# Sliding-window attention into a gated FFT convolution: the inverse transform's complex residues folded about the middle of a block

## The chip, the core and the metric

One core of a Trainium2 chip runs the whole program. The metric is the device time of one execution in microseconds (us), less being better. A core has TensorE (PE in the profile, with its weight loads as PEld), VectorE (DVE), ScalarE (ACT), GpSimd (POOL) and SyncE (SP); each takes its own instructions in order, and they wait for one another by semaphores. In this kernel POOL mostly issues the DMAs that load, and SP those that store or transpose.

## What is computed

Four batches of 768 positions, 8 heads of 64 channels. Each head attends to the last 96 positions and to the first 8, with a bias that falls linearly with distance; its output, as 768 x 512, goes through a projection to three parts x1, x2, x3; x2 is convolved circularly over the 768 positions with a filter, by a Fourier transform; the result is gated by x1 and x3 and projected again.

```python
scores = scale * np.matmul(q, k.transpose(0, 1, 3, 2))
...
a = np.exp(scores)
a = a / (np.sum(a, axis=-1, keepdims=True) + 1e-09)
return np.matmul(a, v).astype(np.float32)
...
proj = x @ w_proj
x1, x2, x3 = (proj[..., :D], proj[..., D:2 * D], proj[..., 2 * D:])
X2 = np.fft.rfft(x2, n=S, axis=1)
H = np.fft.rfft(filter_fft, n=S, axis=0)[None, :, :]
x2_conv = np.fft.irfft(X2 * H, n=S, axis=1)
y = x1 * x2_conv * x3
return (y @ w_out).astype(np.float32)
```

## The kernel before

**Order.** Every piece of work is an operation of a plan (`Plan.op`), and the text `ORDER` writes out the order of all of them by hand: `382P3` is operation 382 on PE into PSUM bank 3, `383A` operation 383 on ACT, V is DVE, G is POOL, S is SP. Many operations may stand on either ACT or DVE (copies out of PSUM, scalings), and the text says which. Words such as `i1b4` are idle products: one 128x512 product (`busy`, L313) whose result nobody reads, put in bank 4. There are 12 of them among the first 66 words and 6 at the very end. The engines follow this order blindly; what is late delays all that stands behind it on its engine.

**Attention, batch b** (`attention`). For batch 0, heads come in pairs: q and k of a pair are loaded, turned on PE (`turned_pair`, L742) and copied to QT and KT. `scores` puts the products of q and k (L809) in two banks; ACT takes their exponential (L821). In batch 0 the bias is added by PE itself (`biased`, L592 to L599, with tables `near` and `edge` that POOL and DVE make from the distances `dg`); in batches 1 to 3 DVE multiplies by a mask (L838). `values` multiplies with v (L857, L862), DVE takes reciprocals (L886) and scales (L881; on ACT L885, in 8 pieces), and x is transposed (PE, L909; batch 3: by DMA, L896). `gate` multiplies with the weights of x1 and x3 (L962, L964), copies x1 out (L321 or L323) and forms g = x1 x3: either ACT copies x3 out first (L976) and DVE multiplies in SBUF, or DVE multiplies straight from PSUM (L978, two forms).

**Convolution, batch b** (`conv`). The transform of 768 positions is split by hand: DVE sums and differences (`butterfly`, L927 to L946) make a real residue and complex residues, `proj` (L1038) multiplies them with the weights of x2, `forward` (L714) with tables `fwd` of sines and cosines, and `spectra` multiplies with the filter's spectrum (L1217 to L1234). The inverse goes, for each of 4 blocks of 128 channels (jp, jj) and for even and odd frequencies (par), through one bank: two products of 256 columns with the tables `inv` (the complex residue, L1066), added up in PSUM, and two of 128 columns with `inr` (the real residue z, L1066 and L1069). The 384 columns are copied to the tile `eo` (ACT L317, mostly). Then `mixed` (DVE, five operations L1168 to L1172, one of which, L1169, may stand on ACT) turns z, u, w into three thirds of a half block, `gated` joins even and odd ones (L1186, L1187) and multiplies by g (L1197), and `out` (L1100) projects; the result is copied (L321 or L323) and stored (L1107). For batches 0 to 2 `mixed` works on all 4 blocks at once (1024 elements per partition), for the last batch on two (512).

**Tables.** `tables` makes the sines: PE forms angles (L503 to L510), ACT and DVE reduce them (L438 to L444), ACT takes the sine (L447). `inverse_tables` transposes six tables on PE (L519, L522) and copies them, scaled, to `inv` and `inr` (six operations on ACT or DVE).

Of the kernel before, what the change touches and what calls it, by code (L numbers as in the profile page):

```python
# [41 lines left out]
0V 3G 14S i1b0 11V 26G i1b1 5V 10V 31G 215P0 7V 1V i1b2 29G 8V 15A i1b3 216A 28G 16V 210P1 217V 13V 6G 218V i1b4 25G  # L42
4V 2A 53V 20V 211A 70P0 27G 9A 212V 100P2 24G 213V 219A i1b5 30G 71V 101A 86P1 44G 84P3 220V 214A i1b6 221V i1b7 85A
87V 18G 58P2 i1b4 i1b0 72P3 12V 21G i1b5 19V 17S i1b1 49V 56P1 255G 50V 202A 54V 52V 73A 51V 92P45 88V 47V 102V 89P67
22G 57A 32G 74V 45V 90P 48V 93P 59V 91A 98P3 33G 75P01 94A 23V 46V 78P67 99V 35G 76P 60A 79P 77A 55V 64P45 36G 61P23
230V 80A 65P 34G 62P 106P01 66A 231V 95P67 38G 63A 96P 107P 232V 103P45 37G 108A 67P23 233V 68P 40G 97A 104P 234V
109P01 222V 39G 105A 235V 112P67 110P 257G 69A 81P45 113V 114V 82P 111A 42G 117P23 236V 127P67 118V 200A 265G 119V
201A 237P0 83A 244P1 128V 264G 129V 122P23 245A 157P45 238A 123V 41G 124V 115P1 130P0 158V 256G 116A 152P67 159V 198A
203A 239P1 254G 131A 153V 125P4 154V 199A 160P5 120P0 253G 223P2 161V 121A 126V 155P3 271G 224V 250P67 156A 143P0 225V
262G 252A 189V 382P3 197A 183V 196A 133P7 263G 251A 209V 190V 142P4 383A 269G 182V 138P6 206V 144A 208V 270G 353P3  # L50
135A 355P4 184V 140A 145V 226V 137P5 43G 356V 227A 354A 351P6 192V 268G 178P4 246A 146V 240A 228V 172P3 487G 139V 241A
247P01 352V 486G 147P5 248A 229V 249V 380P6 174A 258G 149A 148P7 381V 384A 357A 180A 132P5 267G 185V 150A 141V 429P4
186V 134A 273G 191V 367P67 364P01 430V 394P23 368A 167P5 493G 187V 193V 395A 431P4 188V 293P6 194V 500G 204V 169A 195V
365A 177P7 432V 499G 151V 294A 391P45 207V 388P01 385P23 369V 392A 261G 289P6 433V 179V 386A 259S 427P4 266G 290V
278P5 389A 260S 428V 494G 205V 358P67 361P23 396V 437P01 359A 492G 276P4 279V 438A 393V 291P6 274G 277V 362A 173P7
501G 366V 292A 387V 443P23 175A 440P45 272G 434P01 363V 444A 280P6 360V 485G 441A 390V 584P7 370P23 176V 435A 483G
439V 302P4 168P5 303A 495G 402P01 585A 170V 136V 371V 372V 658P4 403V 436V 484G 397P23 281A 404V 609P7 659A 491G 163P6
398V 171V 375P01 445V 498G 165A 162P5 399V 610A 660P4 497G 442V 304P6 446P23 164A 376V 586A 377V 305A 488G 400P5 284P7
447V 401V 378P6 719G 448V 285A 451P01 661A 611P7 181V 727G 379A 452V 449P4 453V 612A 580P5 724G 582P6 450V 373P2 581A
454P3 374V 502G 405P7 662V 242P4 455V 613A 406A 656P2 583V 734G 295P5 166V 657A 297P7 476V 296A 716G 623P23 489S  # L60
593P01 243A 477V 282P6 594A 730G 417P4 490S 298V 624A 407P5 720S 715G 419V 413P7 283A 300V 496G 409A 478V 620P23
663P01 415A 617P45 621A 479V 729G 422P6 306V 412P7 664A 503G 595V 467P2 618A 480V 713G 418P3 424A 414V 469A 714G
596P45 287V 614P67 666P01 597A 665V 522P2 504G 420V 286V 615A 423P4 421V 732G 523A 717S 518P5 299V 667A 718S 275G 598V
590P23 425A 587P67 307V 669P01 731G 519A 509P4 622V 588A 733G 301V 461P5 510A 426V 288V 591A 725G 672P67 408P4 668V
673A 723G 505P2 416V 481V 670A 589V 728G 316P3 320P6 482V 506A 322P7 726G 671V 321A 604P01 308P2 463A 605V 318P6 410V
323A 606V 712G 457P5 317A 592V 309A 314P7 319A 674V 310P3 459A 312P2 619V 315A 533P6 599P01 625V 534A 722G 507P5 600V
311A 411V 601A 313V 735G 680P67 616V 472P4 840S 681V 682V 631P23 474A 626P01 508A 812S 632V 324V 607P6 633A 471P7 325V
456P5 627V 839S 326V 466P4 608V 628A 327V 511P6 838S 513P2 328V 520P3 329V 458A 841S 514A 675P01 521A 330V 683P5 512A
815S 526P3 468A 676V 462P2 677V 527A 531P4 813S 464A 634P6 331V 629P3 684A 602P0 339P2 630A 532V 887S 473A 678P1 332V
524P3 333P7 814S 525A 635V 603V 679A 336P6 516V 340A 811S 705V 334A 845P01 842P23 848P45 846A 460V 342P7 884S 529V  # L70
849A 470V 646P0 465V 843A 847V 885S 636P1 343V 337A 819P23 816P45 535V 648A 886S 641P7 820A 528V 647P0 817A 721S 701P6
649V 475V 530V 638A 650V 345P2 703A 844V 643A 536V 825P01 346A 851P67 888P45 515V 826A 695P3 517V 652P2 889A 706V
686P0 852A 545P1 827V 688A 891P45 708V 822P67 697A 651P0 546A 821V 823A 541P3 707V 696P1 892A 653V 547P6 824V 637P7
548A 709V 698A 549P4 639A 539P5 818V 833P01 542A 710V 537P7 540A 834V 543P3 711V 550A 642P6 544A 538A 828P45 644V 835V
645V 836S 348P3 829V 640V 830A 853V 753P6 344S 654V 893V 551P7 850V 751P0 754A 655V 832S 552A 859P45 349A 553V 854P67
752A 831S 691P3 860V 554V 861A 555V 700P2 350S 855V 685P0 556V 347S 690P1 856V 702A 687A 699V 897P45 862S 557V 894P67
757P0 895A 689V 749P2 558V 837S 898A 755P6 560V 750A 736P7 857S 890V 764P2 737A 740P4 899V 756A 863S 561V 738P5 741A
559V 758A 900P67 341S 693A 858S 896V 765A 577P0 759V 739A 905P23 338S 901V 578A 902V 335S 692A 762P5 742P4 763A 704V
865P1 903S 906V 760V 574P5 867A 907V 904S 744P1 575A 761V 571P0 743A 766V 909S 745A 568P5 572A 746V 565P4 908S 694V
767V 562P0 747V 770P1 748V 563A 774P2 778P3 569A 864P0 930V 566A 570S 772P5 779A 579S 869P4 931V 573S 773A 567S 874P3  # L80
871A 564S 866A 768P5 933V 576S 776P4 780P0 932V 777A 782P6 775A 868V 926P7 934V 783A 781A 941P2 935V 771A 936V 769A
954P6 942A 784V 950P5 955A 785V 786V 952P2 951A 787V 937P6 953V 939P5 788V 938A 876A 789V 965P4 940A 958P6 963P3 959A
791V 956P2 915P5 957A 964A 916P6 961V 966A 943P3 960V 875P2 967V 945P4 962V 920P1 946A 968V 944A 870P0 928A 984P4 947V
877A 880P3 985A 948V 988P2 872A 879P4 949V 989A 975P0 878V 881A 873V 986P2 790V 982P7 917A 971P4 918A 910P5 882V 987A
883V 983A 969P6 972A 973P3 990V 911P7 919V 974A 991V 976A 921P4 913V 992V 970A 792V 922A 925P0 912A 977V 802P1 923A
993V 978A 914V 805P4 927A 994V 979V 929V 808P0 980V 806A 924V 803A 981V 807S 799P7 1010V 809A 1008V 796P6 810S 800A
804S 1009V 793P0 1011V 797A 798S 1015P1 794A 997V 801S 995V 795S 1018P6 1016A 1021P7 996V 1017S 1012P1 998V 1022A
1019V 1005P0 1020S 1013V 1023S 999P6 1014S 1006V 1002P7 1007S 1000V i1b2 1001S 1003A i1b5 i1b3 i1b4 1004S i1b1 i1b0
# [112 lines left out]
class Fused:  # L201
# [12 lines left out]
    DF = ()  # L214
    DI = ()
# [26 lines left out]
    def buffers(self):  # L242
# [23 lines left out]
        self.inv = t("inv", [P, 4, 2, P])  # L266
# [11 lines left out]
        self.eo = t("eo", [P, 4, 2, S // 2])  # L278
# [6 lines left out]
        self.mix = t("mix", [P, 4, 2, P])  # L285
# [3 lines left out]
        self.fwt = t("fwt", [P, 9, P]) if self.DF else None  # L289
        self.fws = t("fws", [P, 10, P]) if self.DF else None  # L290
        self.ivt = t("ivt", [P, 4, 3, P]) if self.DI else None
        self.irt = t("irt", [P, 2, 3, P]) if self.DI else None
        spare = self.eo.rearrange("p a b c -> p (a b c)")
        flat = self.mix.rearrange("p a b c -> p (a b c)")
        self.idle, self.far = flat[:, 0:512], flat[:, 512:728]
        self.edge = flat.bitcast(BF16)[:, 728:896]
# [5 lines left out]
        self.row = spare[0:1, 1984:2624].rearrange("p (a b) -> p a b", a=5)  # L302
# [5 lines left out]
        self.th = [th[:, 0:512], th[:, 512:768]]  # L308
# [78 lines left out]
    def setup(self):  # L387
# [21 lines left out]

        def ident(_):  # L410
            make_identity(nc, self.ident)
# [17 lines left out]
    def tables(self):  # L429

        nc, g, S = self.nc, self.g, self.S
        nf = 2.0 * math.pi / S * (1.0 - 4.0e-7)
        for a, n in enumerate((512, 256)):
            b = g.bank()
            g.op("P", 0.5 if a == 0 else 0.3, lambda _, a=a, b=b: self.angles(a, b.f32()),
                 r=["rows", "irow"], acq=[b], name="angles")
# [479 lines left out]
    def butterfly(self, js):  # L916
# [20 lines left out]
        if self.b in self.DF:  # L937
            return
# [446 lines left out]
```

## Time and profile before

| | us |
|---|---|
| time, median of 3 runs (lowest to highest) | 171.12 (170.71 to 171.39) |
| the profiled execution | 168.81 |
| its span, first to last instruction | 167.1 |
| ACT: exponentials L821, 48 of 920 ns | 40.1 |
| PE: gate products L962, 192 of 326 ns | 36.0 |
| DVE: masks L838, 36 of 597 ns | 20.7 |
| PE: complex residues of the inverse L1066, 64 of 272 ns | 11.4 |
| DMA while POOL loads, 40 to 60 us | 156 to 157 GB/s |

A line such as `L1066 PE MATMUL bank<-inv,X 128*128 128x256 f16 x64 | 11.4, 272` gives the line, the engine, what is written and read, the shape, how many there were, the time that they were busy in all, and the mean ns of one. Products overlap: the time from one start to the next is less than the ns of one. The chain of waits lists what the end waited for, in order of time (start, length, what), and there a group of products has the time from its first start to the next one's.

### The profile page before, as it was taken

To read this page: it belongs to the slowest core of one execution; us is meant where nothing else is said; L and a number is where in the kernel's file an instruction comes from. 1 tells how busy PE (TensorE), PEld (TensorE's weight loads), DVE (VectorE), ACT (ScalarE), POOL (GpSimd) and SP (SyncE) were. 2 spreads that over 40 slices of the span, in tenths; PEclk is the share of its full clock that TensorE was granted. 3 is DMA by queue.
4 is the path that set the end of the run, shared out by engine and by line. 5 is a ranking of instruction groups with operands and counts; after the bars stand their busy time and mean duration, and the time that the engine had idled before them with its cause. 6 is when DMAs were issued, how large, how long until landed. Compare 5 with 4: busy or idle time off the path is not lost.

```text
span 167.1 us, 4421 instructions
## 1 busy us (share of the span) xinstructions
PE 161.8 (97%) x1710; PEld 101.0 (60%) x1710; DVE 151.7 (91%) x345; ACT 141.7 (85%) x290; POOL 74.5 (45%) x96
## 2 busy tenths in 40 slices
PE   6899999999999999999999999999999999999993
PEld 1355588766557785557767556756454754685451
DVE  6965989899999999999999999999997999889980
ACT  7757999899999899999999899988886786698821
POOL 8989598897899999997400000000000000000000
PEclk9999999999999999999999999999999999999999
DMA  2999999999999999999996551024245460000595
GB/s 25 165 194 205 152 177 172 167 154 189 149 155 160 153 150 158 148 160 167 151 152 111 71 108 30 4 78 156 52 144 147 158 246 2 0 4 2 200 346 209
DMA packets 90365, 22.44 MB, mean 134 GB/s; under 512 B 81504, under 2 KB 87400, under 8 KB 90344
## 3 DMA queue, kind: packets, MB, share of 16 engines
q0 software_dynamic: 75296, 12.85, 98.0%
q1 hardware_dynamic: 15048, 9.31, 20.7%
q8 instruction: 13, 0.21, 0.5%
q14 instruction: 8, 0.07, 0.1%
HBM read 25.69 MB, written 6.29 MB: 191 GB/s over the span
## 4 chain that ended last, share of the span: by engine, by line
PE 90%; DMA 5%; POOL 2%; ACT 1%; SPq 0%; issue 0%; POOLq 0%
PE bank L962 19%; PE bank L1100 12%; PE bank L1038 12%; PE bank L809 7%; PE bank L964 6%; PE bank L714 6%; PE bank L1066 5%; PE bank L857 4%; DMA qn<-in_q_dram 3%; PE bank L783 3%; PE bank L862 3%; PE bank L909 3%; PE bank L313 2%; PE bank L592 2%; PE bank L742 2%; DMA xT<-xn 1%
## 5 line engine op out<-in xcount | busy, mean ns | idle before, releaser
L821 ACT ACTIVATE E<-bank 128x864 f16<-128x864 f32 x48 | 40.1, 920 | 1.6 <-PE bank L809 1.5
L962 PE MATMUL bank<-xT,w 128*128 128x384 f16 x192 | 36.0, 326 | 0.0
L333 POOL DMA_DIRECT2D vn<-in_v_dram x28 | 26.4, 957 | 2.4 <-DMA g<-in_moe_filter_fft_dram 1.4
L962 PEld LDWEIGHTS <-w 128*128 128x128 f16 x192 | 17.7, 98 | 11.8 <-issue 0.7
L333 POOL DMA_DIRECT2D kn<-in_k_dram x24 | 21.9, 923 | 2.2 <-PE bank L962 1.3
L1100 PE MATMUL bank<-wo,y 128*128 128x512 f16 (+1 forms) x100 | 22.2, 370 | 0.0
L838 DVE TENSOR_TENSOR E<-E,mask 128x864 f16<-128x864 f16 x36 | 20.7, 597 | 0.1
L333 POOL DMA_DIRECT2D qn<-in_q_dram x21 | 18.9, 910 | 1.1 <-issue 0.6
L321 ACT ACTIVATE ot<-bank 128x512 f32<-128x512 f32 (+1 forms) x20 | 11.3, 596 | 7.1 <-PE bank L1100 7.1
L881 DVE TENSOR_TENSOR xn<-bank,rc 128x512 f16<-128x512 f32 (+1 forms) x19 | 15.2, 800 | 0.4
L1100 PEld LDWEIGHTS <-y 128*128 128x128 f16 x100 | 9.4, 98 | 9.8 <-issue 0.2
L857 PE MATMUL bank<-vn,E 128*128 128x65 f16 x224 | 15.3, 193 | 0.0
L862 PE MATMUL bank<-vn,E 128*128 128x65 f16 x192 | 15.0, 193 | 0.0
L317 ACT CAST X<-bank 128x512 f16<-128x512 f32 x22 | 12.9, 605 | 2.6 <-issue 1.4
L857 PEld LDWEIGHTS <-E 128*128 128x128 f16 x224 | 14.1, 97 | 1.3
L321 ACT ACTIVATE ab<-bank 128x512 f16<-128x512 f32 x20 | 12.6, 629 | 2.1 <-PE bank L1038 2.1
L317 ACT CAST eo<-bank 128x384 f16<-128x384 f32 x31 | 13.9, 521 | 0.5 <-PE bank L1069 0.4
L321 ACT ACTIVATE x<-bank 128x384 f16<-128x384 f32 (+2 forms) x27 | 13.8, 526 | 0.3 <-PE bank L964 0.2
L862 PEld LDWEIGHTS <-E 128*128 128x128 f16 x192 | 13.1, 97 | 1.0
L964 PE MATMUL bank<-xT,w 128*128 128x360 f16 x64 | 12.4, 315 | 0.3 <-DMA xT<-xn 0.3
L809 PE MATMUL bank<-QT,KT 64*128 64x216 f16 (+2 forms) x224 | 12.6, 241 | 0.0
L976 ACT CAST g<-bank 128x384 f16<-128x384 f32 (+2 forms) x23 | 11.2, 512 | 1.3 <-PE bank L964 0.9
(166 smaller groups left out, 366.6 us busy)
## 6 DMA issues: line engine op xcount, KB each, us to landing
out_dram<-ot SPq DMA_DIRECT2D x23, 256.0 KB
vn<-in_v_dram POOLq DMA_DIRECT2D x28, 120.0 KB, 6.3
kn<-in_k_dram POOLq DMA_DIRECT2D x21, 120.0 KB, 6.6
qn<-in_q_dram POOLq DMA_DIRECT2D x18, 128.0 KB, 6.4
w<-in_moe_w_proj_dram POOLq DMA_DIRECT2D x4, 256.0 KB, 7.6
g<-in_moe_filter_fft_dram POOLq DMA_DIRECT2D x1, 768.0 KB, 10.5
qn<-in_q_dram POOLq DMA_DIRECT2D x3, 192.0 KB, 5.8
kn<-in_k_dram POOLq DMA_DIRECT2D x3, 192.0 KB, 5.7
```

The lines of the kernel that those rows point to most:

```text
L317: {"A": nc.scalar.copy, "V": nc.vector.tensor_copy, "G": nc.gpsimd.tensor_copy}[e](out, in_)
L321: self.nc.scalar.mul(out, in_, c)
L333: return self.g.op(eng, 0.57 + 0.00035 * nbytes[0] if eng == "G" else 0.5, lambda _: e.dma_start(dst, src), w=w, r=r, nbytes=nbytes, name= ...
L809: nc.tensor.matmul(bs[hh].f32()[:, off:off + w], self.KT[hs, hp, P * m:P * m + P], self.QT[hs, hp, KL * m:KL * m + w], start=(off == 0 and ...
L821: g.op("A", act(864), lambda _: nc.scalar.activation(eo, bs[0].two()[:, :, 0:432].rearrange("p h (m w) -> p h m w", m=2), Act.Exp, scale=s ...
L838: g.op("V", dve(864, 2), lambda _: nc.vector.tensor_mul(eo, eo, mk), r=[("mask", 2 * hp), ("mask", 2 * hp + 1)] + ([("mask0", hp)], [], [" ...
L857: nc.tensor.matmul(o[:, n, hh], ef[:, at:at + P], vt[:, t, 2 * hp + hh, 0:D + 1], start=first, stop=(t == 0), skip_group_check=True)
L862: nc.tensor.matmul(o[:, n, hh], ef[:, at:at + P], vt[:, t - 1, 2 * hp + hh, 0:D + 1], start=False, stop=True, skip_group_check=True)
L962: nc.tensor.matmul(bk.f32()[:, 0:h], w, self.xT[:, c, lo:lo + h], **kw)
L964: nc.tensor.matmul(bk.f32()[:, 0:360].rearrange("p (t r) -> p t r", t=3), w, self.xTt[:, c, 3 * s:3 * s + 3, 0:KL], skip_group_check=True, ...
L1038: nc.tensor.matmul(bk.f32(), src[:, c], w[:, c, DM:2 * DM], start=(c == 0), stop=(c == 3))
L1100: nc.tensor.matmul(bk.f32()[:, 0:n], y[:, c, P * t:P * t + P], self.wo[:, c, ns], start=(c == 0), stop=(c == 3))
```

## The change

The complex residue of the inverse is evaluated about the middle of each block of 128 positions. At a distance d to both sides of the middle, the cosine part is the same and the sine part has the opposite sign; so PE computes each part for 64 distances only and leaves the two parts apart, and DVE adds and subtracts them.

- **PE.** The bank of one (block, par) takes four products of 128 columns in place of 256, 256, 128 and 128; the two of the complex residue no longer add up (`halves`).
- **DVE.** `mixed` has two new operations ahead: `ma` adds the even and odd parts to columns 64 to 127 of u and w, `mb` subtracts them into columns 63 to 0, written in falling order. The other five stay in number (the scaling is by 0.5 on another tile). `eo` grows from 384 to 640 columns; the tile `mix` is gone, and what it lent room to (the idle products' operand, `far`, `edge`) lies in `eo`.
- **Tables.** `inv` now has 128 columns for each of 4 slots: 64 come from a third group of angles and a third sine, 64 by two scalings on DVE (`other`). PE transposes two whole tables in place of six (the four half transposes stay); three copies to `inr` stay, those to `inv` go.
- **Idle products.** 16 among the first 139 words, one in the middle (among the scores of batch 3), none at the end.
- **Order.** A new `ORDER` throughout: 1055 words in place of 1042. In it 20 operations more stand on ACT, 7 fewer on DVE. The first scores of batch 0 stand behind three of the eight turnings of its pairs (before: behind seven). The third sine stands in the middle of the exponentials of batches 1 and 2, so that ACT loads its tables of functions 5 times in place of 3. POOL issues `ident`, `dg`, `far` and `tail` between the first loads.
- Code that was never reached (dense transforms) is deleted; a few dependences are written more strictly.

```diff
 class Fused:
-        self.inv = t("inv", [P, 4, 2, P])
+        self.inv = t("inv", [P, 4, P])
-        self.eo = t("eo", [P, 4, 2, S // 2])
+        self.eo = t("eo", [P, 4, 2, 5 * P])
-        self.mix = t("mix", [P, 4, 2, P])
-        self.idle, self.far = flat[:, 0:512], flat[:, 512:728]
+        self.idle, self.far = spare[:, 3072:3584], spare[:, 3584:3800]
...
 tables:
+            else:
+                o, th = self.inv[:, :, 0:64], th.rearrange("p (i c) -> p i c", i=4)
+        def other(_):
+            c, t = math.sqrt(0.75), self.inv
+            nc.vector.tensor_scalar(t[:, 0:4:3, 64:P], t[:, 1:3, 0:64], c, None, op0=Alu.mult)
+            nc.vector.tensor_scalar(t[:, 1:3, 64:P], t[:, 0:4:3, 0:64], -c, None, op0=Alu.mult)
...
 inverse_tables:
-            for s in range(6):
-                nc.tensor.transpose(b.f16()[:, P * s:P * s + P], self.fwd[:, s], self.ident)
             for s in range(2):
+                nc.tensor.transpose(b.f16()[:, P * s:P * s + P], self.fwd[:, 4 + s], self.ident)
...
 conv, inverses:
-                        for n, s in enumerate(slots):
-                            z = s >= 4
-                            nc.tensor.matmul(o[:, 0:P] if z else o[:, P:3 * P], X[:, s, cs],
-                                             self.inr[:, s - 4] if z else self.inv[:, (s + 2) % 4],
-                                             start=(n == 0), stop=(n == 1), skip_group_check=True)
-                        nc.tensor.matmul(o[:, 0:P], self.p3[:, par, cs], self.inr[:, 2 + par],
-                                         start=False, stop=True, skip_group_check=True)
+                        self.halves(bk.f32(), cs, slots, par)
...
+    def halves(self, o, cs, slots, par):
+        mm, x = self.nc.tensor.matmul, self.X
+        kw = dict(skip_group_check=True)
+        for n in range(2):
+            mm(o[:, P + P * n:2 * P + P * n], x[:, slots[n], cs], self.inv[:, (slots[n] + 2) % 4], start=(n == 0), stop=True, **kw)
+        mm(o[:, 0:P], x[:, slots[2], cs], self.inr[:, slots[2] - 4], start=False, stop=False, **kw)
+        mm(o[:, 0:P], self.p3[:, par, cs], self.inr[:, 2 + par], start=False, stop=True, **kw)
...
 mixed:
-        z, u, w = (eo[:, :, :, P * m:P * m + P] for m in range(3))
+        z, t, u, w = (eo[:, :, P * m:P * m + P] for m in (0, 1, 3, 4))
+        q = eo[:, :, P:3 * P].rearrange("p a (k c) -> p a k c", k=4)
+        ev, od = q[:, :, 0:4:3], q[:, :, 2:0:-1]
+        uw = eo[:, :, 3 * P:5 * P].rearrange("p a (k c) -> p a k c", k=2)
...
-        op(lambda _: v.tensor_sub(t, z, u), (), "mt")
-        op(lambda e: self.times(e, u, u, 2.0), ("mt",), "mu", 4)
-        op(lambda _: v.tensor_add(z, z, u), ("mt", "mu"), "mz")
-        op(lambda _: v.tensor_sub(u, t, w), ("mt", "mu", "mz"), "m1")
+        op(lambda _: v.tensor_add(uw[:, :, :, 64:P], ev, od), (), "ma")
+        op(lambda _: v.tensor_sub(uw[:, :, :, 63::-1], ev, od), (), "mb")
+        op(lambda e: self.times(e, t, u, 0.5), ("ma", "mb"), "mu", 4)
+        op(lambda _: v.tensor_sub(t, z, t), ("mu",), "mt")
+        op(lambda _: v.tensor_add(z, z, u), ("mt", "ma", "mb"), "mz")
+        op(lambda _: v.tensor_sub(u, t, w), ("mt", "mz"), "m1")
         op(lambda _: v.tensor_add(w, t, w), ("mt", "m1"), "m2")
```

More of the change, by code (lines that the diff above doesn't have):

```diff
@@ L47 @@
[L47 to L56, printed above, removed]
@@ L432, in tables @@
         nf = 2.0 * math.pi / S * (1.0 - 4.0e-7)
-        for a, n in enumerate((512, 256)):
+        for a, n in enumerate((512, 256, 256)):
             b = g.bank()
             g.op("P", 0.5 if a == 0 else 0.3, lambda _, a=a, b=b: self.angles(a, b.f32()),
-                 r=["rows", "irow"], acq=[b], name="angles")
+                 r=["rows", "irow", "jrow"], acq=[b], name="angles")
             th = self.th[a]
@@ L500, in angles @@
         n = P if a == 0 else P // 2
+        o, ph = an[:, 0:4 * n], self.cst[:, None, 0:2, None].to_broadcast([1, 2, 2, n])
+        kw = dict(skip_group_check=True)
+        if a == 2:
+            for f in range(2):
+                nc.tensor.matmul(an[:, P * f:P * f + P], self.row[:, 1 + f], self.row[:, 0:1, 64:P].to_broadcast(
+                    [1, 2, n]), start=(f == 0), stop=False, **kw)
+            nc.tensor.matmul(o, self.one, ph, start=False, stop=True, **kw)
+            return
         fr = self.row[:, 1:3] if a == 0 else self.row[:, 0:4:3, 0:n]
-        nr, o = self.row[:, 4], an[:, 0:4 * n]
@@ L644, in spectrum @@
             b = g.bank()
[L645 removed]
+            keys = lambda i, t: gk + pk + [("fl", (2, 3, 4)[t])]
             if s >= 4:
[L647 removed]
+                self.packed(s, src[s - 4][0], gk + pk + [("fl", 2)], b)
                 continue
[L649 removed]
+            self.forward((s,), lambda i, t: src[i][t], keys, [b])
             pt = b.f32
@@ L693, with forward @@
              ((4, 0),), ((5, 0),)]
-    DENSE = [(2, 8, 10), (3, 11, 9), (0, 12, 14), (1, 13, 15), (4, 4, 4), (5, 16, 5)]
-    def forward(self, ss, src, key, bs, dense=False):
-        if dense:
-            def run3(_):
-                for s, b in zip(ss, bs):
-                    i = 0 if s in (0, 1, 4) else 1
-                    for m, f in enumerate(self.DENSE[s]):
-                        self.nc.tensor.matmul(b.f32(), self.fwd[:, f] if f < 8 else self.fwt[:, f - 8], src(i, m),
-                                              start=(m == 0), stop=(m == 2))
-            self.g.op("P", pe(*[512] * 3 * len(ss)), run3, acq=bs, name="fwd",
-                      r=[k for s in ss for m in range(3) for k in key(0 if s in (0, 1, 4) else 1, m)] + [
-                          ("fwd", 0), ("fwd", 1), "fws"] + [("fwt", o) for o in (0, 2, 4, 6)])
-            return
+    def forward(self, ss, src, key, bs):
         def run(_):
@@ L785, in turned @@
         g.op("P", pe(*[128] * 4 * n), turn, acq=[b], r=["ident"] + [(what + "n", t) for t in ts] + (
-            [("kz", t) for t in ts] if what == "k" and self.b not in self.KG else []), name=what)
+            [("kz", t) for t in ts] if what == "k" else []), name=what)
         lo = NG if what == "k" and self.b in self.KG else 0
@@ L1198, in gated @@
                                                                     gt[:, js, hs]),
-             r=ys + [("g", b % 2, j, x) for j in range(js.start, js.stop) for x in ((0, 1) if half == 0 and b in self.XX else (half,))], w=ys, name="y*g")
+             r=ys + [("g", b % 2, j, x) for j in range(js.start, js.stop) for x in ((0, 1) if half == 0 and (b in self.XX or b + 2 in self.XX) else (half,))], w=ys, name="y*g")
     def spectra(self, b, pair):
```

259 lines of the change are left out of this document (93 added, 166 removed).

## The prediction

> **What bounds the kernel now.** First the page's busy times and its chain of waits.
>
> ```profile
> span 167.1 us, 4421 instructions
> ...
> PE 161.8 (97%) x1710; PEld 101.0 (60%) x1710; DVE 151.7 (91%) x345; ACT 141.7 (85%) x290; POOL 74.5 (45%) x96
> ...
> PE 90%; DMA 5%; POOL 2%; ACT 1%; SPq 0%; issue 0%; POOLq 0%
> ```
>
> PE carries 90% of the chain, but DVE and ACT are close behind. An average hides stages, so next the busy times by stretch (columns: start and end, length, then busy time and count of PE, PEld, DVE, ACT, POOL).
>
> ```profile
> 36.00:60.00 24.00, 24.00 (x312) 16.41 (x310) 23.42 (x58) 22.70 (x41) 22.64 (x26) 1.00 2.27 161
> 60.00:90.00 30.00, 30.00 (x337) 19.57 (x335) 29.75 (x60) 30.00 (x71) 20.13 (x23) 1.00 1.98 150
> 90.00:110.00 20.00, 20.00 (x189) 12.47 (x188) 19.93 (x39) 18.99 (x36) 0.00 (x0) 1.00 0.34 57
> 110.00:130.00 20.00, 19.70 (x178) 10.80 (x176) 18.64 (x39) 15.71 (x40) 0.00 (x0) 1.00 0.42 121
> 130.00:150.00 20.00, 20.00 (x162) 12.95 (x160) 18.73 (x36) 15.94 (x35) 0.00 (x0) 1.00 0.24 85
> 150.00:160.00 10.00, 10.00 (x71) 5.65 (x69) 9.31 (x26) 8.12 (x18) 0.00 (x0) 1.00 0.36 134
> ```
>
> See two stages. From 36 to 110 us all three engines are full: DVE idles 0.58 + 0.25 + 0.07 = 0.90 us, ACT 1.30 + 0 + 1.01 = 2.31. From 110 to 160 PE alone is full: DVE idles 3.32 us, ACT 10.23. PE time saved late comes off the end; saved in the middle, only if DVE and ACT get shorter too.
>
> The front: PE's instructions in order of time (start, length).
>
> ```profile
> 9.56 0.85 PE L742 MATMUL bank<-ident,qn 96*64 96x96 f16 x16
> ...
> 14.19 0.53 PE L742 MATMUL bank<-ident,qn 96*64 96x96 f16 x16
> ...
> 15.59 0.54 PE L809 MATMUL bank<-QT,KT 64*128 64x216 f16 x8
> ```
>
> The first scores run at 15.59, though q and k of one pair were both turned by 10.41 (9.56 + 0.85): ORDER has other turnings in between, and they wait for loads.
>
> **The inverse on PE.** The chain of waits shows what a group costs from start to start, and what a row of 128-column products costs.
>
> ```profile
> 29.04 0.78 PE bank L909 x14
> ...
> 130.23 0.27 PE bank L1066 x3
> 130.51 0.06 PE bank L1069
> 130.56 0.27 PE bank L1066 x3
> ...
> 163.20 1.29 PE bank L313 x6
> ```
>
> A group of the inverse takes 130.56 - 130.23 = 0.33 us. After, it is four products of 128 columns with a weight load each; L909 is a row of just such pairs, 0.78 / 14 = 56 ns apart, so 0.224. Saved: 0.106 x 32 groups = **3.4 us**, 0.85 per batch: 1.7 in the middle stage (batches 0 and 1), 1.7 late (2 and 3). The Trainium skill, TensorE: Matmul & The Clock Gate, section Back-to-back issue gap, says that pairs of load and product at 128 columns come every 81 ns or so; by that a group takes 0.324, and the saving would be 0.2 us. The trace's 56 ns contradicts it here. Four transposes fewer (L519, 0.2 us) and a third group of angles (rows of 0.2 to 0.4 us, in the front where PE waits for loads) cancel. The six idle products at 163.20 start when all useful products have started; the last copy (0.60 us from 163.28) and its store end the span, so removing them brings nothing.
>
> **DVE.** New are `ma` and `mb`: 3 of each with 1024 elements (batches 0 to 2), 2 of each with 512. Rows by shape (count, busy us, mean ns):
>
> ```profile
> L1168 DVE TENSOR_TENSOR mix<-eo 128x1024 f16<-128x1024 f16 x3 | 2.0, 674 | 0.4 <-ACT eo L317 0.4
> L881 DVE TENSOR_TENSOR xn<-bank,rc 128x768 f16<-128x768 f32 x8 | 7.6, 954 | 0.2
> L978 DVE TENSOR_TENSOR g<-bank,x 128x384 f16<-128x384 f32 x7 | 3.7, 534 | 0.0
> L978 DVE TENSOR_TENSOR g<-g,x 128x384 f16<-128x384 f16 x17 | 5.8, 345 | 0.0
> ```
>
> At the rate of L1168 (and its 420 ns at 512) `ma` and `mb` cost 3 x 2 x 0.68 + 2 x 2 x 0.42 = 5.8 us. `mb` writes backwards, which no row shows. Its lower bound is the forward row; its upper one the slow rate of L881 and L978, 420 ns for 384 elements more, so 1.23 us at 1024 and 0.68 at 512: 2.2 us more. I take the lower: same type, same tile, and L1234, which reads its two blocks in reverse order, takes 686 ns. Counting both orders instruction by instruction, DVE also gains two scalings of `xn` (2 x 0.69), two copies of keys (2 x 0.64) and small ones (2.1 together), and loses 8 gatings from PSUM (534 - 345 = 0.19 us each, 1.5), five table copies (1.5), two copies of X (1.4), two of `ab` (1.4), two of `ot` (1.1), one of `x1` (0.5) and five half scalings (1.8): 4.8 - 9.2 = -4.4 us. Net **+1.4 us**, up to +3.6.
>
> **ACT** takes what DVE drops: 8 copies of g (4.1), five half scalings (4.1, estimated from the 0.69 us of the one now on ACT and the 1.0 of a 960-element copy), X, `ab`, `ot`, `x1` (4.0), three copies to `inr` instead of one (0.8), a third sine and its angles (0.8); it drops 16 small scalings of `xn` (8.6 / 40 x 16 = 3.4), key copies (3.0) and small ones (1.0). And it loads function tables twice more:
>
> ```profile
> L607 ACT ACT_TABLE_LOAD x1 | 1.3, 1283 | 0.3 <-DVE dg L552 0.3
> ```
>
> 2 x 1.28 = 2.6 us; the next instruction starts as the load ends (3.42 + 1.28 to 4.71 for L392). The Trainium skill, ScalarE: Activation LUTs, section What ACT_TABLE_LOAD costs, adds a drain and comes to 2.66 us per switch; by it the two would cost 5.3. The trace shows no drain. Net for ACT, with the traced 2.6: **+9.0 us**.
>
> **Sum by stage.**
> - *Front.* The 12 exponentials of batch 0 run from 15.99 to 26.3. In the new order ACT's work from its table load for them to the twelfth is 1.28 + 12 x 0.80 (their spacing, 7.16 / 9) + six masks 2.2 + copies 3.3 = 16.4 us, and the load can start when the second sine ends: 8.84 before, about 9.5 with its angles later. So the twelfth ends at 25.9, with five masks more done (1.9 us). Gain 0.4 + 1.9 = 2.3 if loads keep up; `dg`, `far` and `tail` on POOL (1.2 + 0.6 + 0.2 us) now delay the last pair's load by 2.0 us, which eats part: bounds 0 and 2.3. I take 1.5. The denser idle products fill waits; at nothing, 8 of them behind the first scores cost 0.22 each (1.7) where PE does not wait.
> - *Middle.* PE -1.7. ACT +3.6 here (table loads 2.6, gatings 2.5, the sine, `inr` and one `mix` 2.2, X, `ab` and `ot` 2.4; less 3.4 for `xn`, 2.0 for keys, 0.6), against 2.31 of idle: 1.3 too much. DVE +0.4 to +1.9, against 0.90. So PE's gain is not collected. I put the stretch 1.0 us longer, between -1.7 (absorbed by the earlier front) and +2.3 (both surpluses, 1.3 + 1.0, one behind the other).
> - *Late.* PE -1.7; DVE +0.2 (`ma`, `mb` 3.0, less `ab`, `ot`, gatings and scalings 2.8) against 3.3 of idle, ACT +3 against 10.2. Collected. Behind the last inverse PE has four gate groups and six projections, 4 x 0.68 + 5.2 = 7.9 us (before 7.2); DVE's work from that group's copy (1.3 us) to the first gated half is 6.3: covered by 0.3.
>
> -1.5 + 1.0 - 1.7 = **-2.2 us**: 168.81 becomes 166.6 in a profiled execution (span 164.9, the 1.7 around it kept). The median of the runs, 171.12, lies 2.3 above the profiled execution; I carry the difference over: **168.9**.
>
> **Rivals.**
> 1. *Everything is collected*: the middle shrinks with PE because the earlier front feeds it: -2.3 - 3.4 = -5.7, 165.4. For it: ACT's busy time in 36 to 110 contains waits that overlap; a copy of 384 columns takes 526 ns alone, 0.40 in a row (2.39 for 6 at 134.08). Against: ACT is at 30.00 of 30 already. 0.15.
> 2. *Engines give all of it back*: DVE and ACT set the pace in the middle and the front gains nothing, 171 within 1.2. For it: 99% on both. 0.18.
> 3. *Slower*: ACT overflows in 60 to 90 us. Two table loads and a sine stand between exponentials; while they run (2.6 us) exponentials are late, each holds two of eight banks, and PE stops for want of banks. Price: loads 2.6 in full with the 1.3 surplus, less 1.7 late, the front's gain lost in the jam: 171.12 + 2.2 = 173.3. It decides if ACT's surplus there exceeds its 2.31 of idle and nothing moves out. 0.15.
> 4. *`mb` runs at the slow rate*: +2.2 on DVE, half in the middle, half before the last projections with 0.3 of cover: 168.9 + 2.2 = 171.1. 0.09.
> 5. *Short products gain nothing* (the change doesn't do what it says): with the weight load exposed, 98 ns each in the PEld rows, a group takes 0.39, +0.06 x 32 = 1.9 above before: 173.0. L909 speaks against it. 0.03; the page's 81 ns belongs here.
>
> My forecast, 168.9 (167.4 to 170.3), has 0.40. A measurement of this kernel can tell some 0.5% (0.86 us) from no change. Faster: 0.15 + 0.38 + 0.04 of rival 2 = 0.57; within: 0.20; slower: 0.15 + 0.03 and ends of 2 and 4 = 0.23. The range, with one in ten left out on each side, reaches into rivals 1 and 3: 165.5 to 173.2.
>
> **What would show it.** Groups of the inverse 0.22 us apart; `mb` at 0.68 or 1.23 us; ACT busy near 150, DVE near 153; first exponential near 11 us; PE idle or spread out between 60 and 90 us while ACT is full (rival 3 when much); the last useful product at about 161. I am wrong if PE stays dense throughout, or if the front's loads come later than I think.

## The result, and the profile after

The changed kernel takes 172.73 us (median; 171.31 to 174.02), beside 170.26 for the kernel before on the same chip: ratio 1.0144, 95% interval 1.012 to 1.0167. It is slower by 2.5 us; the forecast was 168.9 (167.4 to 170.3), faster by 2.2. The profiled execution takes 173.15 us.

First the page of the changed kernel: the span, each engine's busy time, and the engines' shares of the chain of waits.

```profile
span 171.4 us, 4437 instructions
...
PE 162.5 (95%) x1708; PEld 97.6 (57%) x1708; DVE 151.5 (88%) x350; ACT 148.1 (86%) x296; POOL 74.6 (44%) x96
...
PE 57%; DVE 25%; ACT 7%; DMA 6%; issue 2%; SPq 1%; POOL 0%; DVEq 0%; ACTq 0%; POOLq 0%
```

PE's share of the chain fell from 90% to 57%: something now makes PE wait. The windows (start and end, length, then busy time and count of PE, PEld, DVE, ACT, POOL) say where.

```profile
36.00:60.00 24.00, 24.00 (x279) 14.99 (x278) 22.45 (x53) 23.73 (x42) 19.21 (x22) 1.00 2.21 162
60.00:90.00 30.00, 30.00 (x345) 19.52 (x346) 29.69 (x62) 28.92 (x61) 24.28 (x27) 1.00 2.01 140
90.00:110.00 20.00, 17.51 (x164) 10.29 (x162) 18.31 (x35) 17.17 (x32) 0.00 (x0) 1.00 0.56 98
110.00:130.00 20.00, 20.00 (x224) 12.23 (x223) 19.09 (x41) 19.14 (x48) 0.00 (x0) 1.00 0.28 82
130.00:150.00 20.00, 18.97 (x126) 10.41 (x125) 18.21 (x35) 16.79 (x36) 0.00 (x0) 1.00 0.30 98
```

PE loses 2.49 us from 90 to 110, at the end of the stage that the prediction calls the middle, and 1.03 from 130 to 150, in the late stage, where I had expected its saved time to be collected. From 60 to 90, rival 3's place, it has no gap. The waits (engine and line, releaser: us in total, times, longest) name what it waited for:

```profile
PEld L759 <- DMA KT<-kn: 2.1, 1, 2.1
PE bank L759 <- DMA KT<-kn: 1.6, 1, 1.6
DVE xab L881 <- DMA xT<-xn: 1.5, 1, 1.5
PE bank L912 <- DMA xT<-xn: 1.0, 1, 1.0
SPq L327 <- DMA kn<-in_k_dram: 16.2, 1, 16.2
```

The first four lines are batch 3's scores, which wait for its transposed k, and its sums and gates, which wait for its transposed x. Both are transposed by DMAs that SP issues, and the last line is SP itself, waiting for a load of keys before its copies `kn<-kn`. Here are SP's DMAs of the changed kernel in order of time (start, length of the row from first to last, line, out<-in, count):

```profile
85.25 1.42 SPq L327 DMA_DIRECT2D kn<-kn  x2
86.86 5.33 SPq L721 DMA_TRANSPOSE QT<-qn  x4
92.30 6.25 SPq L721 DMA_TRANSPOSE KT<-kn  x4
...
116.00 1.17 SPq L846 DMA_TRANSPOSE xT<-xn  x1
117.23 1.54 SPq L1041 DMA_DIRECT2D out_dram<-ot  x3
118.81 6.03 SPq L846 DMA_TRANSPOSE xT<-xn  x4
124.89 0.57 SPq L1041 DMA_DIRECT2D out_dram<-ot  x1
125.51 8.95 SPq L846 DMA_TRANSPOSE xT<-xn  x7
```

SP issues one transpose per 1.2 to 1.3 us (8.95 / 7). The first stands behind the copies of the global keys, which wait for the first keys of batch 3 (the 16.2 us above); in the kernel before these copies were issued at 69.34 us and the first transpose at 81.65, here at 85.25 and 86.86. SP is through with the last transpose of x at 134.46 (before 129.95), the projection of batch 3 starts at 139.21 (before 135.25), and the useful products are through 4.3 us later than before (167.53, before 163.20).

The fold itself does what the prediction said. PE's rows in order of time, and DVE's two new operations by shape:

```profile
136.28 0.28 PE L1064 MATMUL bank<-inv,X 128*128 128x128 f16 x2
136.39 0.22 PE L1065 MATMUL bank<-inr,X 128*128 128x128 f16 x1
136.44 0.22 PE L1066 MATMUL bank<-inr,p 128*128 128x128 f16 x1
136.50 0.27 PE L1064 MATMUL bank<-inv,X 128*128 128x128 f16 x2
```

```profile
L1096 DVE TENSOR_TENSOR eo<-eo 128x1024 f16<-128x1024 f16 x3 | 2.1, 685 | 0.0
L1097 DVE TENSOR_TENSOR eo<-eo 128x1024 f16<-128x1024 f16 x3 | 2.0, 673 | 0.0
```

Groups are 136.50 - 136.28 = 0.22 us apart (rival 5 falls), and `mb` (L1097), which writes backwards, takes 673 ns, no more than `ma` (rival 4 falls).

The front, again PE's rows: turnings (L692) and scores (L759).

```profile
8.34 0.85 PE L692 MATMUL bank<-ident,ab 96*64 96x96 f16 x16
...
10.48 0.54 PE L759 MATMUL bank<-QT,KT 64*128 64x216 f16 x4
...
13.27 0.85 PE L692 MATMUL bank<-ident,kn 96*64 96x96 f16 x16
...
14.60 0.54 PE L759 MATMUL bank<-QT,KT 64*128 64x216 f16 x4
...
15.61 0.53 PE L692 MATMUL bank<-ident,ab 96*64 96x96 f16 x16
```

The first scores come 5.1 us earlier than before (15.59), but the second ones follow 4.1 us behind them, and ACT idles 1.91 us before its second exponential. No load holds them: PE is busy 4.00 us of 8 to 12 and 4.00 of 12 to 16. It works there at a slow rate, 0.85 us for sixteen turnings at 13.27 and 0.53 at 15.61, and idle products, biases and a turning stand between the first scores and the second. In e7 below, whose front has the same instructions in the same order, PE was at its full rate by 10.57 us, and the second exponential started at 12.98 without a wait (here 15.18). The twelfth ends at 27.47 (before 26.33), and batch 0's first gate product starts at 34.89 (before 31.09). Not all of these 3.8 us are lateness: 24 turnings of batch 1 (some 1.3 us by their rows) stand ahead of that gate in the new order and stood behind it before.

### The profile page after: what moved, and what is told of

The parts are those of the page before. It is cut to its first block, busy times and chain, and to the rows that moved or that the text cites. A ratio compares the mean times of both kernels' runs of the same rounds, so it can differ in the third digit from the quotient of the medians.

```text
span 171.4 us, 4437 instructions
## 1 busy us (share of the span) xinstructions
PE 162.5 (95%) x1708; PEld 97.6 (57%) x1708; DVE 151.5 (88%) x350; ACT 148.1 (86%) x296; POOL 74.6 (44%) x96
## 4 chain that ended last, share of the span: by engine, by line
PE 57%; DVE 25%; ACT 7%; DMA 6%; issue 2%; SPq 1%; POOL 0%; DVEq 0%; ACTq 0%; POOLq 0%
PE bank L910 12%; PE bank L1034 8%; PE bank L984 6%; ACT E L771 5%; PE bank L759 5%; PE bank L912 4%; DVE E L788 4%; PE bank L733 3%; DVE xn L831 3%; PE bank L664 3%; PE bank L692 3%; PE bank L307 2%; DMA KT<-kn 2%; DMA kn<-in_k_dram 2%; PE bank L859 2%
## 5 line engine op out<-in xcount | busy, mean ns | idle before, releaser
L771 ACT ACTIVATE E<-bank 128x864 f16<-128x864 f32 x48 | 40.8, 910 | 5.3 <-PE bank L759 5.1
L327 POOL DMA_DIRECT2D vn<-in_v_dram x28 | 25.5, 913 | 4.4 <-PE bank L812 3.0
L1034 PE MATMUL bank<-wo,y 128*128 128x512 f16 (+1 forms) x100 | 22.9, 370 | 0.0
L924 ACT CAST g<-bank 128x384 f16<-128x384 f32 (+2 forms) x31 | 15.2, 509 | 1.6 <-PE bank L912 1.2
L759 PE MATMUL bank<-QT,KT 64*128 64x216 f16 (+2 forms) x224 | 14.4, 246 | 2.2 <-DMA KT<-kn 1.6
L831 DVE TENSOR_TENSOR xn<-bank,rc 128x512 f16<-128x512 f32 (+1 forms) x21 | 16.3, 783 | 0.1
L315 ACT ACTIVATE ot<-bank 128x512 f32<-128x512 f32 (+1 forms) x22 | 12.8, 594 | 4.0 <-PE bank L1034 3.4
L807 PE MATMUL bank<-vn,E 128*128 128x65 f16 x224 | 15.7, 193 | 0.1
L812 PE MATMUL bank<-vn,E 128*128 128x65 f16 x192 | 15.4, 193 | 0.0
L311 ACT CAST X<-bank 128x512 f16<-128x512 f32 x24 | 13.5, 598 | 2.2 <-PE bank L664 2.1
L759 PEld LDWEIGHTS <-KT 64*128 64x128 f16 x224 | 7.8, 94 | 10.1 <-issue 6.2
```

Of the source, the lines that this page charges most:

```text
L311: {"A": nc.scalar.copy, "V": nc.vector.tensor_copy, "G": nc.gpsimd.tensor_copy}[e](out, in_)
L315: self.nc.scalar.mul(out, in_, c)
L327: return self.g.op(eng, 0.57 + 0.00035 * nbytes[0] if eng == "G" else 0.5, lambda _: e.dma_start(dst, src), w=w, r=r, nbytes=nbytes, name= ...
L759: nc.tensor.matmul(bs[hh].f32()[:, off:off + w], self.KT[hs, hp, P * m:P * m + P], self.QT[hs, hp, KL * m:KL * m + w], start=(off == 0 and ...
L771: g.op("A", act(864), lambda _: nc.scalar.activation(eo, bs[0].two()[:, :, 0:432].rearrange("p h (m w) -> p h m w", m=2), Act.Exp, scale=s ...
L807: nc.tensor.matmul(o[:, n, hh], ef[:, at:at + P], vt[:, t, 2 * hp + hh, 0:D + 1], start=first, stop=(t == 0), skip_group_check=True)
```

## The experiments

The theories: **A**, the fold is sound and the new order costs; **B**, the fold's work on DVE and ACT costs more than PE saves; later **C**, within A: the late loads and transposes of batch 3. Ratios are to the kernel before on the same chip, with 95% intervals; 0.01 is 1.7 us.

**e1 and e2: one half of the change each.** `ORDER` of the one kernel is carried over to the other, operation by operation.

```diff
-ORDER of the changed kernel
+ORDER of the kernel before; new operations beside their relatives
+5V 6V ... 211P1 221P5 ... 212A 222A ... 214V 223V 224V ... 215A 225A ... 231A 226V
```

> The folded inverse in the order of the kernel before: each operation stands where its counterpart stood, the new ones (third angles and sine, the two of the mixing, the scaled tables) next to their relatives, the six idle products at the end left out. Theory A (the fold is sound, the new order costs): PE saves up to 3.4 us, DVE gains 5.8 us of which the late stage hides its part, so 1 to 3 us below the kernel before (ratio 0.982 to 0.994). Theory B (the fold's own work on DVE and ACT costs more than PE saves): 0.5 to 2.5 us above it (ratio 1.003 to 1.015), like the changed kernel.

173.5 us, ratio 1.0198 (1.0163 to 1.0234). B's side, and above even B's range.

> The unfolded inverse in the new order (each operation at its counterpart's place; no third angles and sine, so three loads of function tables; six table copies again). Theory A: the order costs 4 to 6 us by itself, so 2 to 6 us above the kernel before (ratio 1.015 to 1.035), above the changed kernel too. Theory B: without the fold's work the new order is no slower than the old one, ratio 0.99 to 1.005.

173.37 us, 1.0217 (1.0193 to 1.024). A's number. So neither half is a gain alone: by the ratios the order costs 3.7 us, and the fold in the old order 3.4. In the new order the fold takes 0.7% off (1.0217 to 1.0144). The page of e1 shows why it fails in the old order:

```profile
PE 161.2 (94%) x1703; PEld 98.7 (57%) x1703; DVE 157.5 (92%) x358; ACT 142.4 (83%) x292; POOL 74.6 (43%) x96
...
PE 47%; DVE 37%; DMA 5%; issue 3%; ACT 3%; POOL 2%; SPq 0%; ACTq 0%; POOLq 0%
```

DVE has 5.8 us more than before (151.7), the size of `ma` and `mb`, and takes 37% of the chain. The first exponential starts at 17.07 us (before 15.99). The third group of angles is not shown to be the cause: a turning that waits for its keys starts at 9.03 (before 8.57), and the rest comes with PE's slow rate, 0.85 us for sixteen turnings at 13.52 (before 0.66 at 13.06). In e8, in the same order, the first exponential starts at 17.63.

**e3 and e4: old front with new rest, and the reverse.** Spliced at batch 0's first gate product.

> The changed kernel with the old order up to the first gate product of batch 0 and the new order from there on. If the front carries the loss (first gate 3.8 us late), 2.5 to 4 us below the changed kernel, ratio to the kernel before 0.990 to 1.000. If the loss is made later (late loads and transposes of batch 3), within 1 us of the changed kernel, ratio 1.008 to 1.018.

176.83 us, 1.0416 (1.0377 to 1.0455).

> The folded inverse with the new order up to the first gate product of batch 0 and the old order from there on. If the front carries the loss: about the changed kernel's time, ratio to the kernel before 1.005 to 1.020. If the loss is made later: below the kernel before, ratio 0.982 to 0.997.

189.57 us, 1.1173 (1.1146 to 1.12). Both fall outside both of their expected ranges and are slower than either whole order, so they tell nothing of the front: the first gate product, 31 to 35 us in the whole orders, came at 38.4 and 39.5 us. An order cut in two makes jams of its own.

**e5: batch 3's loads by use.** POOL's words of batch 3 in another order, and the copies of the global keys (726, 725) early on SP.

```diff
-743G 720G 737G 724G 731G 742G 741G 739G 721G 730G 727G 740G 723G 733G 722G 738G 735G 734G 732G 736G
+720G 723G 721G 722G 724G 733G 739G 740G 731G 732G 734G 737G 738G 727G 730G 735G 736G 741G 742G 743G
```

> The changed kernel, but POOL issues the loads of batch 3 in the order in which they are used (q and k ahead, values last), and SP's two copies of the global keys stand behind the first of them, in place of at 85 us. Theory C (late loads and late DMA transposes of batch 3 set the end of the new order): POOL loses its 3.0 us stall at 60 us, the transposes of q and k start 4 to 6 us earlier, PE's waits before the first scores of batch 3 (1.6 + 0.6 us) go, and the time falls by 1.5 to 3 us (ratio to the kernel before 0.997 to 1.006). Rival: DVE and ACT are what is late behind them; then the scores only wait elsewhere, and the time stays within 0.7 us of the changed kernel (ratio 1.010 to 1.018).

169.38 us, 0.996 (0.9933 to 0.9986): 1.8%, or 3.1 us, below the changed kernel, and below the kernel before. C holds. SP's DMAs of e5:

```profile
66.80 1.88 SPq L327 DMA_DIRECT2D kn<-kn  x2
69.28 17.10 SPq L721 DMA_TRANSPOSE QT<-qn  x4
86.54 5.55 SPq L721 DMA_TRANSPOSE KT<-kn  x4
92.20 2.51 SPq L721 DMA_TRANSPOSE QT<-qn  x2
```

SP is through with the first eight transposes at 92.1 in place of 98.5 us, and PE's gap from 90 to 110 us shrinks from 2.49 to 0.15 us, as e5's windows show:

```profile
90.00:100.00 10.00, 9.85 (x99) 5.58 (x98) 10.00 (x22) 9.53 (x19) 0.00 (x0) 1.00 1.21 129
100.00:110.00 10.00, 10.00 (x89) 5.91 (x86) 9.86 (x18) 9.93 (x20) 0.00 (x0) 1.00 0.14 42
```

**e14 and e15: which part of e5.** e14 moves only the first keys (723) to the second place, with 726 and 725 behind them; e15 moves only 743, which stalls POOL for 3.04 us, to the end.

> The changed kernel with only the first keys of batch 3 moved from the 13th to the 2nd place among its loads, and SP's two copies of the global keys behind them; POOL's stall at 60 us stays. If it is the place of these keys that costs (13 transposes wait behind them on SP): 2 to 3 us below the changed kernel, ratio 0.996 to 1.003. If it is POOL's stall, which delays all loads: within 0.8 us of it, ratio 1.010 to 1.017.

173.11 us, 1.019 (1.0142 to 1.0238).

> The changed kernel with only the load that stalls POOL for 3.0 us at 60 us moved behind the other loads of batch 3, so that all others come 3 us earlier; the first keys stay behind the others. If POOL's stall costs: 2 to 3 us below the changed kernel, ratio 0.996 to 1.003. If the place of the keys costs: within 0.8 us of it, ratio 1.010 to 1.017.

172.83 us, 1.0166 (1.0126 to 1.0205). Neither alone gains anything. The next row of e14's SP, and of e15's POOL (start, length, idle time ahead), show what took the place:

```profile
68.37 1.47 SPq L327 DMA_DIRECT2D kn<-kn  x2
70.04 22.28 SPq L721 DMA_TRANSPOSE QT<-qn  x4
92.48 6.07 SPq L721 DMA_TRANSPOSE KT<-kn  x4
```

```profile
62.03 0.89 POOL L327 DMA_DIRECT2D qn<-in_q_dram  x1 [3.27 <-PE bank L859]
```

In e14 the four transposes of q take until 92.3 us; SP waits 17.1 us for loads of q, because some of the queries are still issued last, at 79 and 84 us, behind values that no product needs before 114 us. In e15 a load of queries stalls POOL in 743's place. So the last load that a transpose needs counts, and my reading is that all of q and k have to stand ahead of the values, as in e5; no run tests less than e5's whole reordering with success.

**e9, e10 and e18: the fold once the loads are repaired.** e9 is e5 with the old inverse. e10 is e5 with four stores of batch 0 (347, 344, 350, 341), ready by 107.4 us, ahead of the first transpose of x; e18 is e10 with the old inverse.

```diff
-847S 347S 344S 350S 846S 872S 873S 868S 341S 867S
+347S 344S 350S 341S 847S 846S 872S 873S 868S 867S
```

> The unfolded inverse in the new order, with the loads of batch 3 in the order of their use (as in the run of that name with the fold, 169.4 us, ratio 0.996). With the late loads out of the way the fold shows its own worth: if it is worth its PE time there (up to 3.4 us), this is 1 to 3 us above that run (ratio 1.002 to 1.014). If DVE and ACT hand it back (rival 2 of the prediction), it is within 0.7 us of it (0.992 to 1.000).

172.07 us, 1.0118 (1.0075 to 1.016).

> The fold in the new order with the loads by use, and four stores of batch 0's output, ready by 107.4 us, issued on SP ahead of the first transpose of batch 3's x (112.5 us) and not among these transposes, where they take 2.1 us of SP's queue. If that queue sets the end from there (PE and DVE wait 1.0 and 1.5 us for its last transposes), the last transpose starts 1 to 2 us earlier and the time falls by 0.7 to 1.7 us (ratio 0.986 to 0.992). If not: within 0.5 us of 169.4 (0.993 to 0.999).

168.13 us, 0.99 (0.9855 to 0.9944), an interval that touches that of e5; e13 and e17 below, which contain the same move, lie there too. DVE's wait for the transposed x, 1.5 us in e5 as in the changed kernel, is 0.2 us in e10. SP's rows of e10: the twelve transposes of x are one row, and SP is through with the last 1.6 us earlier than in e5 (129.4, there 131.0).

```profile
102.97 5.01 SPq L1041 DMA_DIRECT2D out_dram<-ot  x5
112.23 17.15 SPq L846 DMA_TRANSPOSE xT<-xn  x12
```

> The unfolded inverse in the new order with the loads by use and the stores ahead. If the stores are the rest of what the order costs: 1.2 us below e9, ratio 1.003 to 1.007, and the fold is worth some 2.5 us in this order. If something else remains: 1.009 to 1.014.

171.47 us, 1.0085 (1.0053 to 1.0117). With both repairs the fold is worth 1.0085 - 0.99 = 1.85%, 3.1 us (by the two intervals, 1.9 to 4.5): about the 3.4 us worked out for PE. It is the net of all that the fold changes, its work on DVE and its tables too. With the first alone it is 1.0118 - 0.996 = 1.6%, 2.7 us; in the new order as it came 1.2. The loads by use are in turn worth 1.7 us without the fold (1.0217 to 1.0118), and 3.1 with it. The 0.85% that e18 still lies above the kernel before is what is left of the order's cost; its cause stays open.

**e7 and e8: the two new DVE operations cut short**, in the new and in the old order. Each is cut to 2 columns of one block, so the residues are left folded; the later operations read other columns of the tile, in the same shapes.

```diff
-        op(lambda _: v.tensor_add(uw[:, :, :, 64:P], ev, od), (), "ma")
+        op(lambda _: v.tensor_add(uw[:, 0:1, :, 64:66], ev[:, 0:1, :, 0:2], od[:, 0:1, :, 0:2]), (), "ma")
```

> The changed kernel with the two new operations of the mixing cut to 2 columns of one block each (the residues are then not unfolded; the later operations of the mixing read other columns of the same tile, in the same shapes). DVE has 5 us less. If order and loads set the end (theory A and C): within 1 us of the changed kernel, ratio to the kernel before 1.007 to 1.018. If DVE's unfolding is what is paid (theory B): 3 to 5 us less, ratio 0.985 to 0.997.

171.8 us, 1.0119 (1.0082 to 1.0155): 4.3 us of DVE's work (147.2 us busy, in the changed kernel 151.5) cost 0.4 us by the ratios in the new order, and the intervals overlap.

> The fold in the old order, with the two new operations cut in the same way. In that run (173.5 us) DVE was busy 157.5 us, and the lateness grew from 1.1 us at the first exponential to 4.9 us at the last product. If DVE's unfolding makes that growth: 3 to 5 us below it, at or below the kernel before (ratio 0.985 to 1.002). If not: within 1 us of it (1.014 to 1.022).

169.79 us, 0.997 (0.9939 to 1.0001): in the old order the same work (4.8 us; 152.7 us busy, in e1 157.5) costs 3.9 us. In that order DVE had no room for it. Without it the fold still gains no more than 0.3% there, within the interval, and not PE's 3.4 us; what holds the rest back stays open. The new order has 5.8 us less on DVE (145.9 us in e2, before 151.7), and there the fold's work fits in.

**e16: the old order with the new order's choice of engine** for every operation that may stand on either.

> The fold in the old order (173.5 us, ratio 1.020), with every operation that may stand on ACT or DVE on the engine that the new order gives it: 42 from DVE to ACT, 24 from ACT to DVE, so that DVE has some 6 us less and ACT 5 us more. If the fold failed in the old order only for want of DVE's time: 2 to 4 us less, ratio 0.995 to 1.008. If the old order's sequence does not fit the moved work: no better, ratio 1.015 or above.

184.39 us, 1.0861 (1.0807 to 1.0915). The theory that the moved work alone is what the old order lacked is not borne out: sequence and choice of engine belong together.

**e6 and e12: the front.** I took the turning ahead of the second scores to wait for a load, which the trace does not show. e6 moves these scores (91P) ahead of that turning (59P) and weights and keys ahead of batch 1's queries on POOL; e12 is e5 with the first swap alone.

> The changed kernel with two swaps in the front: the second scores of batch 0 ahead of the turning of k that waits for the fourth load, and POOL's loads of weights and of keys ahead of the queries that wait 3.3 us for the last turning. If the front's 3.8 us of lateness at the first gate are carried to the end: ACT's 1.9 us of idle time before the second exponential go, POOL gains 2 to 3 us, and the time falls by 1.5 to 3 us (ratio 0.997 to 1.006). If later stages set the end: the first gate comes 1 to 2 us earlier, the end within 0.7 us of the changed kernel (1.010 to 1.018).

176.29 us, 1.0371 (1.0337 to 1.0405). The second swap made the queries late: PE's turnings of batch 1 waited 2.4 us for them (`DMA qn`), and the first gate came at 38.4 us. It answers neither of its expectations.

> The fold in the new order with the loads by use, and in the front only one swap: the second scores of batch 0 ahead of the turning that waits for the fourth load. If the front's lateness is carried to the end: 0.7 to 1.5 us less (ratio 0.987 to 0.992). If it is absorbed: within 0.6 us of 169.4 (0.993 to 1.000).

169.37 us, 0.9963 (0.9936 to 0.999): the same as e5. The second exponential starts at 13.30 us without a wait (e5: 14.36), the twelfth ends 0.3 us earlier, and the first gate comes at 33.87 (e5: 33.89). As the gate did not move, this says that the second exponential's lateness costs nothing that can be told, and not what an earlier gate would bring.

**e11, e13 and e17: function tables and idle products.** e11 is e5 with the third angles and sine beside the first two; e13 is e10 with that; e17 is e10 without its 17 idle products.

> The fold in the new order with the loads by use, and the third angles and sine beside the first two, so that ACT loads its function tables three times and not five. If the two extra loads cost (rival 3's term): ACT has 2.6 us less between 54 and 62 us, the first exponential comes about 0.8 us later, and the time falls by 0.7 to 1.8 us (ratio 0.986 to 0.992). If ACT's loads lie beside other work: within 0.6 us or up to 1 us slower (0.993 to 1.003).

169.12 us, 0.9946 (0.9919 to 0.9973).

> The fold in the new order with three repairs: loads of batch 3 by use, the four stores ahead of the transposes, the third angles and sine beside the first two. If the repairs add up: 0.25 us below the run with the stores ahead (168.1 us, ratio 0.990), so 0.985 to 0.990. If the earlier sine only delays the first exponential once the queue of SP is free: 0.990 to 0.996.

168.1 us, 0.9883 (0.9844 to 0.9921).

> The fold in the new order with the loads by use and the stores ahead (168.1 us, ratio 0.990), without its 17 idle products. If they only fill waits (costed at nothing): within 0.6 us, 0.987 to 0.994. If they hold useful products up in the front (0.22 us each, 8 behind the first scores): up to 1.7 us faster, 0.980 to 0.987. If they bring PE to its full rate earlier: 1 us or more slower, 0.996 or above.

167.78 us, 0.9892 (0.9851 to 0.9934). Two table loads fewer take 2.5 us off ACT (145.2, in e5 147.7) and bring some 0.25 us, which the intervals cannot tell from nothing; the idle products bring and cost nothing that can be told. e10, e13 and e17 are the fastest, 1.0 to 1.2% below the kernel before.

## Why the prediction was wrong, step by step

- **The missing term: loads and SP's queue.** The step that failed is the sum by stage. It counted PE, DVE and ACT, and followed POOL in the front alone. It never looked where the new order puts batch 3's loads on POOL or the transposes and stores on SP, though nearly all of them had moved. That is worth 3.1 us (e5), and the stores some 1.0 us more (e10, with intervals that touch). Without the two the change would have been 168.1 us, ratio 0.990, by chance near the forecast (168.9 beside 171.12, 0.987), for the front and the middle did not go as forecast. Nor do the 2.3 us from the profiled execution to the median carry over: they come to 170.26 - 168.81 = 1.45 before and to 172.73 - 173.15 = -0.4 after.
- **Late, -1.7 for PE.** The size was about right: 3.1 against 3.4 us, for the whole kernel and net, are collected in e10 against e18. It failed as "collected" because from 90 us on the end hung on SP's transposes, which PE's savings do not touch: there the fold brought 1.2 us.
- **The page's 81 ns.** By the Trainium skill, TensorE: Matmul & The Clock Gate, section Back-to-back issue gap, the fold would have saved an estimated 0.2 us; the trace's 0.22 us per group and e18 against e10 contradict it here.
- **Front, -1.5.** Not borne out. The first exponential came 4.9 us earlier, near the forecast of 11 us. But the sum took ACT's work as the bound, and ACT waited for PE, whose slow rate was no term of it; the idle products put at 0.22 us each take 0.4 to 0.5 there (1.06 us for the two at 12.28). The twelfth ended 1.1 us later than before in this profile. In five other profiles with the same front it ended at 25.4 (e7), 26.2 (e10), 26.4 (e5), 27.1 (e14) and 27.3 us (e15), later the later PE came to its full rate, with 25.9 forecast. The first gate started at 33.1 to 34.4 in these five. Whether the end pays for that is not shown: with the gate at 33.89, e5 ends batch 0's output at 110.1 us (before 110.7), and no run has the new order with an earlier gate than 33.1.
- **Middle, +1.0, and rival 3.** Rival 3's 173.3 is nearest to the result, and its mechanism is not what happened: PE has no gap from 60 to 90 us, ACT, which the sum had 1.3 us too full, idles 0.27 + 1.08 + 2.83 = 4.2 us from 36 to 110, and with the two table loads gone the time falls by some 0.25 us, within the intervals. What this stage lost is PE's 2.49 us at its end, for the transposed k. The Trainium skill, ScalarE: Activation LUTs, section What ACT_TABLE_LOAD costs, would make it 5.3 us for the two, an estimate; the trace has 1283 ns for each and no drain, and e11 shows that they lie beside other work.
- **DVE and ACT.** DVE was put at +1.4 us and measured -0.2; ACT at +9.0 and measured +6.4. That `ma` and `mb` take 5.8 us came out (5.7), and in an order with DVE full they cost 3.9 (e8). Rival 2, in which DVE and ACT hand the saving back, falls for DVE in the new order: without this work the time falls by 0.4 us (e7).
- **Edits costed at nothing.** The idle products: right for the end (e17). "The third group of angles cancels against the transposes" stays open: the later first exponential of e1 has other causes in the trace, a later load and PE's later change of rate.

## What to carry to other kernels

When an order is rewritten, follow every queue in it to the first consumer, the DMA queues too: here loads that nobody needed yet stood ahead of queries and keys on POOL, and so held up SP's transposes. A saving on one engine shows in full only once what ends last is repaired, so measure it there (e10 against e18) before it is thrown away. And read the start of a kernel from several executions: one profile can have PE slow for 5 us longer than another. Parts of two hand-made orders did not mix: the three mixtures here (e3, e4, e16) were slower than every whole order.

## What the runs showed of the hardware

PE came to its full rate late, and at a time that differs from one execution to the next, though the granted clock reads 1.00 throughout. The idle products show it, being the same 128x512 product each time. In the changed kernel:

```profile
7.80 0.61 PE L307 MATMUL bank<-eo 128*128 128x512 f16 x1
...
15.07 0.61 PE L307 MATMUL bank<-eo 128*128 128x512 f16 x1
...
18.06 0.38 PE L307 MATMUL bank<-eo 128*128 128x512 f16 x1
```

In e7, with the same instructions in the same order up to there:

```profile
7.90 0.61 PE L307 MATMUL bank<-eo 128*128 128x512 f16 x1
...
10.57 0.39 PE L307 MATMUL bank<-eo 128*128 128x512 f16 x1
```

PE was as busy in both (3.86 us of 4 to 8 and 4.00 of 8 to 12; in e7 3.75 and 4.00). In e5, e10, e14 and e15, with the same front, the change lies between 12.2 and 15.1 us. So a single trace can't tell whether denser work brings it forward; e17, without idle products, has the slow 0.84 for sixteen turnings at 14.27 still. The Trainium skill, TensorE: Matmul & The Clock Gate, section What you observe, has the change at around 4 us of sustained work; the traces differ, with PE busy almost without a gap from 1.3 us on and a spread of 5 us. What it is worth in the total stays open: in e11's profiled execution PE is at its full rate by 7.25 us, and it took 168.71 us, where the runs of e11 take 168.71 to 169.95.
